# Scaling blocks of probabilities on GpSimd too, with priorities shifted by a fixed table, in an attention and gated feed-forward kernel

## The chip, the cores and the metric

The kernel runs on one core of a Trainium2 chip. The metric is the device time of one execution in microseconds (us), as the median of several runs. A core has TensorE (PE: matmuls and transposes, with PEld for its weight loads), VectorE (DVE), ScalarE (ACT), GpSimd (POOL) and SyncE (SP), which here issues all DMAs. Each engine works through its own list of instructions in order; they meet at semaphores.

## The reference

Windowed causal attention with a linear position bias is followed by a gated feed-forward layer. There are 8 batches of 8 heads, 576 tokens and 64 dimensions a head; then 4608 tokens of 512 go through 1536 hidden channels.

```python
scores = scale * np.matmul(q, k.transpose(0, 1, 3, 2))
mask = (rel >= 0) & (rel < window)               # window = 128
scores = np.where(mask, scores + bias[None], -1000000000.0)
attn = np.exp(scores - np.max(scores, axis=-1, keepdims=True))
attn = attn / (np.sum(attn, axis=-1, keepdims=True) + 1e-09)
attn_out = np.matmul(attn, v)
x = attn_out.transpose(0, 2, 1, 3).reshape(B * S, H * D)
gate = 1.0 / (1.0 + np.exp(-(x @ w_gate)))
out = gate * (x @ w_val) @ w_out
```

## The kernel before

**Attention.** A unit is one batch and one pair of heads, so there are 32 units of 2 x 576 = 1152 tokens, or nine blocks of 128. TensorE computes scores for four blocks at a time (L388), VectorE folds the two halves of the window (L396), adds the bias and takes the minimum of the negated scores (L404), and ScalarE takes the exp with its sum (L407). Three blocks form a group: VectorE adds a small number to the three sums (L422) and takes their reciprocals (L424), and then each of the three 128x128 blocks is multiplied by its own column of reciprocals, on ScalarE (L427) or VectorE (L428). This multiplication is called scaling below. TensorE transposes the three blocks (L432), ScalarE or VectorE copies them out of PSUM (tile both, L205 and L206), and GpSimd spreads them by two selects into pt (L443). After three groups TensorE multiplies with the values (L469 in the first eight units, L493 later), and the result goes to xt and to DRAM; from unit 8 on VectorE adds a second part to it (L505).

**Feed-forward.** All of it runs in pieces that were split into a high and a low part, with three matmuls for a product. A third of the hidden channels is computed while attention runs (gates1, matmul L550, 480 of them); its input x is split from xt or read back (x<-xt, x<-xr), its weights are decoded by ScalarE and VectorE (L303, L304, L307, L215). The rest is done after attention by seven products of combined blocks in place of eight (gates2, L635; mixed inputs cxA, cxB, cxC), and then the output projection (results, L761).

**What sets the order.** Every instruction is first recorded with an engine, a cost, what it reads and writes, and a wanted time (want). `order` then plays the engines forward: of the operations whose inputs are ready it takes the one that can start first, in steps of 0.05 us, and among equals the one with the smaller want. An operation with `ways` may go to another engine at that engine's cost; `port` keeps VectorE and GpSimd from planned work on SBUF at once. The programs are issued in the order of planned starts. In the first 30 us of the plan, gaps of TensorE are filled with matmuls of the identity matrix (L265). The attention operations want a time that advances with the unit (6.5 us each for the first eight, 10 us each later); gates1's matmuls want a million and so fill what is left; scores, transposes and values of unit 8 and later are planned 0.5 us after their inputs. Before the play, `shift` groups the operations by their want and moves some groups:

```python
for seed in SEEDS:
    rnd = random.Random(seed)
    share, width = rnd.choice((5, 20, 60)), rnd.choice((0.7, 2.0, 6.0))
    for group in rnd.sample(groups, max(1, len(groups) // share)):
        shift = rnd.gauss(0.0, width)
```

Of the kernel before, what the change touches and what calls it, by code (L numbers as in the profile page):

```python
# [2 lines left out]

# [47 lines left out]
YIELD = {"DVE": 0.1, "POOL": 0.0}  # L51
NRAW = 2
SOON = 150.0
SEEDS = (36, 163, 243, 291, 310, 1168, 1444)


def as32(ap):
# [7 lines left out]
class Graph:  # L65
# [87 lines left out]
    def shift(self):  # L153

        groups = {}
        for o in self.ops:
            groups.setdefault((o.want, o.seq // 40 if abs(o.want) > 1e5 else 0), []).append(o)
        groups = list(groups.values())
        for seed in SEEDS:
            rnd = random.Random(seed)  # L160
            share, width = rnd.choice((5, 20, 60)), rnd.choice((0.7, 2.0, 6.0))
            for group in rnd.sample(groups, max(1, len(groups) // share)):
                shift = rnd.gauss(0.0, width)
                for o in group:
                    o.want += shift

    def play(self):
        self.fill = []
# [15 lines left out]
def attention_gated_ffn(ctx: ExitStack, tc: tile.TileContext, qd, kd, vd, wg, wv, wo, out):  # L184
    nc = tc.nc
# [230 lines left out]
    def probabilities(u, i0):  # L416
# [8 lines left out]
        for e in range(n):  # L425
            args = lambda e=e: (pb()[:, e], pb()[:, e], st()[:, 6 + e:7 + e])
            g.add("ACT", 0.3, lambda args=args: nc.scalar.mul(*args()), [(kst, 6)], [(kpb, e)], want,  # L427
                  ways=[("DVE", 0.196, True, lambda args=args: nc.vector.tensor_scalar_mul(*args()))])  # L428

        def transpose():  # L430
            for e in range(n):
# [555 lines left out]
```

## Time and profile before

| | |
|---|---|
| median of 3 runs | 974.3 us (974.27 to 975.93) |
| span of the profiled execution | 971.9 us |
| busy share of TensorE, VectorE, ScalarE, GpSimd | 99%, 83%, 54%, 14% |
| attention stage, to the first matmul L635 | 0 to 286.6 us |
| gates2, to the first matmul L761 | 286.6 to 707.6 us |
| results, to the end of TensorE | 707.6 to 968.0 us |
| granted clock of TensorE | 1.00 in every slice |

The profile shows one execution. Its page gives the busy share of each engine; the other views list groups of instructions by line, stretches of time, waits, or the instructions one after another. Durations on ScalarE and VectorE hold a tail that overlaps the next instruction, and ends of matmuls are modelled, so that the distance from one start to the next is the safer price of a matmul.

### The profile page before, as it was taken

To read this page: it belongs to the slowest core of one execution; us is meant where nothing else is said; L and a number is where in the kernel's file an instruction comes from. 1 tells how busy PE (TensorE), PEld (TensorE's weight loads), DVE (VectorE), ACT (ScalarE), POOL (GpSimd) and SP (SyncE) were. 2 spreads that over 40 slices of the span, in tenths; PEclk is the share of its full clock that TensorE was granted. 3 is DMA by queue.
4 is the path that set the end of the run, shared out by engine and by line. 5 is a ranking of instruction groups with operands and counts; after the bars stand their busy time and mean duration, and the time that the engine had idled before them with its cause. 6 is when DMAs were issued, how large, how long until landed. Compare 5 with 4: busy or idle time off the path is not lost.

```text
span 971.9 us, 18577 instructions
## 1 busy us (share of the span) xinstructions
PE 963.7 (99%) x6574; PEld 818.5 (84%) x6574; DVE 808.1 (83%) x1948; ACT 523.9 (54%) x1383; POOL 138.6 (14%) x237
## 2 busy tenths in 40 slices
PE   9999999999999999999999999999999999999998
PEld 7678777777788889999988888888888999988886
DVE  7998989988969998894789439796999779898882
ACT  7999998799945555453444333532463144332320
POOL 5343443234410110000001000010100000000000
PEclk9999999999999999999999999999999999999999
DMA  8776679676635448752154211436345244637101
GB/s 313 223 267 236 226 241 317 213 247 215 221 111 154 168 156 271 227 189 94 50 189 139 100 65 66 140 125 222 102 153 189 93 141 136 228 98 238 44 23 65
DMA packets 83612, 162.68 MB, mean 167 GB/s; under 512 B 9408, under 2 KB 35008, under 8 KB 83520
## 3 DMA queue, kind: packets, MB, share of 16 engines
q1 hardware_dynamic: 83520, 161.51, 49.9%
q8 instruction: 51, 0.84, 0.4%
q14 instruction: 41, 0.34, 0.1%
HBM read 111.15 MB, written 50.33 MB: 166 GB/s over the span
## 4 chain that ended last, share of the span: by engine, by line
PE 87%; DVE 8%; ACT 3%; DMA 1%; issue 1%; POOL 0%; ACTq 0%; POOLq 0%; SPq 0%; DVEq 0%
PE mm L635 40%; PE mm L761 27%; PE mm L550 8%; PE mm L388 5%; PE mm L493 3%; PE mm L432 3%; DVE work L307 1%; ACT pb L407 1%; DMA xr<-xs 1%; DVE pb L404 1%; ACT pb L427 1%; PE mm L469 1%; DVE mm L396 1%; DMA hs<-ring 0%; PE mm L265 0%
## 5 line engine op out<-in xcount | busy, mean ns | idle before, releaser
L635 PE MATMUL mm<-cxB,w2s 128*128 128x512 f32 (+1 forms) x684 | 159.1, 372 | 0.1
L635 PE MATMUL mm<-cxA,w2s 128*128 128x512 f32 (+1 forms) x684 | 159.1, 372 | 0.0
L205 ACT COPY ring<-mm 128x512 f32<-128x512 f32 (+1 forms) x141 | 77.1, 554 | 129.7 <-PE mm L635 101.1
L635 PEld LDWEIGHTS mm<-cxB,w2s 128*128 128x128 f32 x684 | 125.5, 188 | 18.7 <-ACT ring L205 0.5
L635 PEld LDWEIGHTS mm<-cxA,w2s 128*128 128x128 f32 x684 | 125.8, 188 | 18.4
L550 PE MATMUL mm<-x,w 128*128 128x512 f32 x480 | 139.1, 414 | 1.7 <-DVE x L215 1.0
L443 POOL TENSOR_SCALAR_AFFINE_SELECT pt<-both 128x384 f32<-128x384 f32 x192 | 103.6, 564 | 160.8 <-ACT both L205 151.1
L407 ACT ACTIVATE pb<-pb,st 128x128 f32<-128x128 f32 x288 | 112.9, 397 | 9.6 <-DVE st L404 9.2
L761 PE MATMUL mm<-cxA,wos 128*128 128x512 f32 (+1 forms) x540 | 113.7, 367 | 0.0
L761 PE MATMUL mm<-cxB,wos 128*128 128x512 f32 (+1 forms) x540 | 113.3, 367 | 0.0
L761 PEld LDWEIGHTS mm<-cxA,wos 128*128 128x128 f32 x540 | 98.4, 188 | 12.7
L761 PEld LDWEIGHTS mm<-cxB,wos 128*128 128x128 f32 x540 | 98.3, 188 | 12.6
L550 PEld LDWEIGHTS mm<-x,w 128*128 128x128 f32 x480 | 84.4, 188 | 23.6 <-issue 5.3
L646 ACT ACTIVATE sg<-mm 128x512 f32<-128x512 f32 (+1 forms) x96 | 53.9, 564 | 79.7 <-PE mm L635 37.8
L642 DVE TENSOR_TENSOR mm<-mm,ring 128x512 f32<-128x512 f32 (+1 forms) x96 | 62.3, 649 | 31.7 <-PE mm L635 28.2
L214 POOL TENSOR_TENSOR work<-work 128x256 f32<-128x256 f32 x29 | 23.5, 815 | 390.4 <-DVE work L307 282.7
L307 DVE SCALAR_TENSOR_TENSOR work<-work 128x512 int32<-128x512 int32 x104 | 71.5, 701 | 0.6
L427 ACT ACTIVATE pb<-pb,st 128x128 f32<-128x128 f32 x198 | 67.8, 396 | 6.1 <-DVE st L424 5.2
L404 DVE CUSTOM_DVE_ANT_0 pb<-mm,relm 128x128 f32<-128x128 f32 x288 | 67.7, 280 | 0.0
L388 PE MATMUL mm<-kr,qr 64*64 64x192 f32 (+2 forms) x1280 | 67.2, 322 | 0.0
L772 ACT ACTIVATE ring<-mm 128x512 f32<-128x512 f32 (+2 forms) x41 | 22.3, 546 | 82.9 <-PE mm L761 79.7
L388 PEld LDWEIGHTS mm<-kr,qr 64*64 64x64 f32 x1280 | 43.1, 133 | 21.3 <-issue 16.2
(111 smaller groups left out, 1553.8 us busy)
## 6 DMA issues: line engine op xcount, KB each, us to landing
hs<-ring SPq DMA_DIRECT2D x72, 256.0 KB, 2.1
kr<-in_k_dram SPq DMA_DIRECT2D x31, 576.0 KB, 5.0
work<-in_moe_w_gate_dram SPq DMA_DIRECT2D x20, 512.0 KB, 3.9
work<-in_moe_w_val_dram SPq DMA_DIRECT2D x20, 512.0 KB, 4.5
qr<-in_q_dram SPq DMA_DIRECT2D x31, 320.0 KB, 5.4
vr<-in_v_dram SPq DMA_DIRECT2D x32, 288.0 KB, 3.5
xs<-xt SPq DMA_DIRECT2D x32, 288.0 KB, 3.2
hr<-hs SPq DMA_DIRECT2D x18, 512.0 KB, 4.7
```

What stands on the lines that cost most here:

```text
L205: g.add("ACT", act_cost(n, psum), lambda: nc.scalar.copy(out(), src()), reads, writes, want, release=release, ways=[("DVE", dve_cost(n, ps ...
L307: g.add("DVE", dve_cost(DM, two=True), lambda word=word, scalar=scalar, o0=o0: nc.vector.scalar_tensor_tensor(bits(), wraw(s)[:, :, word], ...
L388: nc.tensor.matmul(sp[j // 2][col, j % 2, c0:c0 + n], qraw(u)[row, i // 2, col], kraw(u)[row, k1:k1 + n], start=True, stop=True)
L404: g.add("DVE", 0.21, lambda: nc.vector.tensor_tensor_reduce(pb()[:, e], sp[j // 2][:, j % 2, D:D + P], relm[u.p][:, w], op0=ALU.add, op1=A ...
L407: g.add("ACT", 0.39, lambda: nc.scalar.activation(pb()[:, e], pb()[:, e], AF.Exp, bias=st()[:, e:e + 1], scale=-1.0, accum_out=st()[:, 3 + ...
L427: g.add("ACT", 0.3, lambda args=args: nc.scalar.mul(*args()), [(kst, 6)], [(kpb, e)], want, ways=[("DVE", 0.196, True, lambda args=args: n ...
L443: nc.gpsimd.affine_select(pt(u)[:, f0:f0 + 2 * n - 1:2, :], both(), [[0, n], step], cmp, 0.0, base=0, channel_multiplier=mult)
L550: nc.tensor.matmul(mm[s][:, 0:n], w1(kind, wi)[:, i, c * P:(c + 1) * P], x1(x)[:, c, 0:n], start=(k == 0 and c == 0), stop=(k == 2 and c = ...
L635: nc.tensor.matmul(mm[b][:, 0:N], w2t(i, wp)[:, wk, c * P:(c + 1) * P], combo(k, xp)[:, c, 0:N], start=(start and c == 0 and j == 0), stop ...
L642: g.add("DVE", dve_cost(N, psum=True), lambda: nc.vector.tensor_tensor(o(), bk(b)(), a(), op=ALU.add), [("mm", b), *reads] if okeys else r ...
L646: g.add("ACT", act_cost(N, psum=True), lambda: nc.scalar.activation(sg[h](), bk(b)(), AF.Tanh, scale=0.5), [("mm", b)], [("sg", h)], F)
L761: nc.tensor.matmul(mm[banks_[i]][:, a:b], wot(e * HC + c, wp)[:, k, i * P:(i + 1) * P], hcombo(s, xp)[:, c, a:b], start=(start and e == c ...
```

## The change

Two things change. A scaling may also be planned on GpSimd, at a cost of 0.42 us in the plan, where ScalarE has 0.3 and VectorE 0.196. And `shift` moves the groups by a fixed table of tenths of a microsecond in place of the draws.

```diff
-SEEDS = (36, 163, 243, 291, 310, 1168, 1444)
+SHIFTS = (
+    (2, -27), (3, 4), (4, -5), (5, -4), (6, -10), (7, 3), (8, 7), (9, 13), (10, 11), (12, -44), (14, -3), (15, -8), (16, 5), (17, -56), (18, 4),
...
-        for seed in SEEDS:
-            rnd = random.Random(seed)
-            share, width = rnd.choice((5, 20, 60)), rnd.choice((0.7, 2.0, 6.0))
-            for group in rnd.sample(groups, max(1, len(groups) // share)):
-                shift = rnd.gauss(0.0, width)
-                for o in group:
-                    o.want += shift
+        for k, tenths in SHIFTS:
+            for o in groups[k]:
+                o.want += tenths / 10
...
             g.add("ACT", 0.3, lambda args=args: nc.scalar.mul(*args()), [(kst, 6)], [(kpb, e)], want,
-                  ways=[("DVE", 0.196, True, lambda args=args: nc.vector.tensor_scalar_mul(*args()))])
+                  ways=[("DVE", 0.196, True, lambda args=args: nc.vector.tensor_scalar_mul(*args())),
+                    ("POOL", 0.42, True, lambda args=args: nc.gpsimd.tensor_scalar_mul(*args()))])
```

What this does to the programs is shown at three places. In the new kernel the lines of this part are 18 or 19 higher: selects are L462, scalings L445 (ScalarE), L446 (VectorE) and L447 (GpSimd), exps L425, gates1's matmuls L569, gates2's L654.

GpSimd in the first two units: pb is a block of probabilities, st its sums and reciprocals, both the transposed group, pt the spread one. Before:

```order
L443 AFFINE_SELECT pt_270<-both_261 128x3x128 x2
L443 AFFINE_SELECT pt_270<-both_299 128x3x128 x2
L443 AFFINE_SELECT pt_270<-both_329 128x3x128 x2
L443 AFFINE_SELECT pt_404<-both_261 128x3x128 x2
L443 AFFINE_SELECT pt_404<-both_299 128x3x128 x2
L443 AFFINE_SELECT pt_404<-both_329 128x3x128 x2
```

and now:

```order
L447 TENSOR_SCALAR pb_192<-pb_192,st_193 128x128
L462 AFFINE_SELECT pt_262<-both_251 128x3x128 x2
L462 AFFINE_SELECT pt_262<-both_289 128x3x128 x2
L447 TENSOR_SCALAR pb_270<-pb_270,st_271 128x128
L462 AFFINE_SELECT pt_262<-both_334 128x3x128 x2
L462 AFFINE_SELECT pt_372<-both_251 128x3x128 x2
L447 TENSOR_SCALAR pb_307<-pb_307,st_308 128x128
L447 TENSOR_SCALAR pb_318<-pb_318,st_319 128x128
L462 AFFINE_SELECT pt_372<-both_289 128x3x128 x2
L462 AFFINE_SELECT pt_372<-both_334 128x3x128 x2
L447 TENSOR_SCALAR pb_369<-pb_369,st_370 128x128
L447 TENSOR_SCALAR pb_415<-pb_415,st_416 128x128
```

Scalings of later units stand between the selects of the older ones. The new program has 88 of them on GpSimd.

ScalarE in the first units: exps (L407, now L425), scalings (L427, now L445) and copies of transposed groups. Before, from the first scaling of unit 2 on:

```order
L427 ACTIVATE pb_302<-pb_302,st_303 128x128 x2
L427 ACTIVATE pb_311<-pb_311,st_312 128x128 x2
L407 ACTIVATE pb_364,st_365<-pb_364,st_365 128x128
L205 COPY both_299<-mm_146 128x384
L407 ACTIVATE pb_415,st_416<-pb_415,st_416 128x128 x3
L427 ACTIVATE pb_311<-pb_311,st_312 128x128
L427 ACTIVATE pb_364<-pb_364,st_365 128x128 x3
L205 COPY both_329<-mm_146 128x384
L427 ACTIVATE pb_415<-pb_415,st_416 128x128
L407 ACTIVATE pb_192,st_462<-pb_192,st_462 128x128 x3
L407 ACTIVATE pb_200,st_472<-pb_200,st_472 128x128
L427 ACTIVATE pb_415<-pb_415,st_416 128x128 x2
```

and now, at the same place:

```order
L445 ACTIVATE pb_307<-pb_307,st_308 128x128
L445 ACTIVATE pb_318<-pb_318,st_319 128x128 x2
L223 CAST x_413<-xt_394 128x512
L223 COPY both_289<-mm_146 128x384
L425 ACTIVATE pb_369,st_370<-pb_369,st_370 128x128
L425 ACTIVATE pb_415,st_416<-pb_415,st_416 128x128 x3
L223 COPY both_334<-mm_146 128x384
L445 ACTIVATE pb_369<-pb_369,st_370 128x128
L425 ACTIVATE pb_192,st_458<-pb_192,st_458 128x128 x3
L425 ACTIVATE pb_200,st_467<-pb_200,st_467 128x128
L445 ACTIVATE pb_369<-pb_369,st_370 128x128
L445 ACTIVATE pb_415<-pb_415,st_416 128x128 x2
```

Of scalings there are 198 before and 151 now. In this stretch ScalarE also has a cast of x from xt, which VectorE did. VectorE has 90 scalings before and 49 now.

TensorE at the end of attention, from the last matmuls of the last values on (pt, vr), over the remaining matmuls of gates1 (x, w) to the first of gates2 (cxA). Before:

```order
L493 MATMUL mm_146<-pt_404,vr_180 64x64 x4
L550 MATMUL mm_141<-x_396,w_524 128x512 x12
L550 MATMUL mm_140<-x_396,w_524 128x512 x7
L550 MATMUL mm_141<-x_396,w_524 128x512 x4
L550 MATMUL mm_140<-x_396,w_524 128x512 x12
L550 MATMUL mm_141<-x_396,w_524 128x512 x8
L635 MATMUL mm_140<-cxA,w2s_2461 128x512 x6
L635 MATMUL mm_143<-cxA,w2s_2626 128x512 x6
L635 MATMUL mm_146<-cxA,w2s_4146 128x512 x6
```

and now:

```order
L512 MATMUL mm_146<-pt_372,vr_180 64x64 x4
L569 MATMUL mm_141<-x_413,w_527 128x512 x3
L569 MATMUL mm_140<-x_413,w_527 128x512 x6
L569 MATMUL mm_141<-x_413,w_527 128x512 x12
L569 MATMUL mm_140<-x_413,w_527 128x512 x6
L654 MATMUL mm_143<-cxA,w2s_2707 128x512 x6
L569 MATMUL mm_140<-x_413,w_527 128x512 x12
L569 MATMUL mm_141<-x_413,w_527 128x512 x12
L654 MATMUL mm_140<-cxA,w2s_2507 128x512 x6
L654 MATMUL mm_142<-cxA,w2s_2507 128x512 x6
```

The first six matmuls of gates2 moved ahead of the last 24 of gates1. There are 51 matmuls of gates1 behind the last values now, and there were 43; over the whole stage the 480 stand in 97 runs now and in 106 before, and 33 identity matmuls stand in the program where 32 stood.

## Rows read from the trace of the kernel before

**Rows 1.** the page, engines' busy time over the whole span.
```profile
PE 963.7 (99%) x6574; PEld 818.5 (84%) x6574; DVE 808.1 (83%) x1948; ACT 523.9 (54%) x1383; POOL 138.6 (14%) x237
```

**Rows 2.** Stretches: us; busy PE, PEld, DVE, ACT, POOL (instructions); clock; DMA share; GB/s.
```profile
0.00:50.00 50.00, 47.47 (x497) 35.62 (x498) 43.19 (x212) 42.82 (x168) 22.09 (x41) 1.00 0.80 269
50.00:287.00 237.00, 235.43 (x2799) 185.08 (x2798) 211.41 (x980) 209.06 (x790) 88.62 (x166) 1.00 0.69 229
287.00:708.00 421.00, 420.78 (x2011) 367.49 (x2011) 338.86 (x525) 187.46 (x320) 27.88 (x32) 1.00 0.44 145
```

**Rows 3.** timeline, TensorE and VectorE, attention's end: start, length, what.
```profile
276.60 10.17 PE L550 MATMUL mm<-x,w 128*128 128x512 f32 x43
286.61 2.65 PE L635 MATMUL mm<-cxA,w2s 128*128 128x512 f32 x11
...
279.99 0.69 DVE L206 CAST cxC<-xr 128x1024 fp32r<-128x1024 f32 x1 [2.18 <-DMA xs<-xt]
```

**Rows 4.** groups of TensorE in 0 to 50 us: busy, mean ns, idle before.
```profile
L265 PE MATMUL mm<-ident 128*128 128x128 f32 x64 | 9.2, 284 | 0.0
L270 PE MATMUL mm<-ident 128*128 128x128 f32 x12 | 2.9, 434 | 1.4 <-POOL ident masks.py:199 1.4
```

**Rows 5.** stretch of 25 to 50 us, columns as in rows 2.
```profile
25.00:50.00 25.00, 23.89 (x251) 16.32 (x250) 23.45 (x110) 24.11 (x96) 9.57 (x18) 1.00 0.73 229
```

**Rows 6.** waits of the attention stage: who for whom, us, times, longest.
```profile
PEld mm L432 <- ACT both L205: 2.1, 6, 0.7
PEld mm L469 <- POOL pt L443: 0.6, 2, 0.4
POOL pt L443 <- ACT both L205: 151.1, 83, 9.9
```

**Rows 7.** timeline of TensorE: start, length, what.
```profile
19.00 0.55 PE L432 MATMUL mm<-ident,pb 128*128 128x128 f32 x3
19.47 0.88 PE L388 MATMUL mm<-kr,qr 64*64 64x192 f32 x16
...
213.85 1.62 PE L550 MATMUL mm<-x,w 128*128 128x512 f32 x6
215.31 0.49 PE L432 MATMUL mm<-ident,pb 128*128 128x128 f32 x3
215.56 0.47 PE L550 MATMUL mm<-x,w 128*128 128x512 f32 x1
215.96 0.88 PE L388 MATMUL mm<-kr,qr 64*64 64x192 f32 x16
```

**Rows 8.** groups by line and shape, whole span: busy, mean ns, idle before.
```profile
L427 ACT ACTIVATE pb<-pb,st 128x128 f32<-128x128 f32 x198 | 67.8, 396 | 6.1 <-DVE st L424 5.2 <-DVE st L422 0.7
L205 ACT CAST x<-xr 128x512 fp32r<-128x512 f32 x6 | 3.7, 611 | 0.0
...
L428 DVE TENSOR_SCALAR pb<-pb,st 128x128 f32<-128x128 f32 x90 | 24.0, 302 | 0.2
L422 DVE TENSOR_SCALAR st<-st 128x3 f32<-128x3 f32 x96 | 20.6, 215 | 7.9 <-ACT pb L407 6.7
L206 DVE CAST w<-work 128x512 fp32r<-128x512 f32 x8 | 3.6, 459 | 0.0
...
L443 POOL TENSOR_SCALAR_AFFINE_SELECT pt<-both 128x384 f32<-128x384 f32 x192 | 103.6, 564 | 160.8 <-ACT both L205 151.1 <-DVE both L206 4.6 <-PE mm L388 4.2
L248 POOL TENSOR_SCALAR relm<-relm 128x640 f32<-128x640 f32 x3 | 5.4, 1812 | 1.9 <-DVE relm L243 1.7
```

**Rows 9.** L422's and L428's durations; pairs of selects on GpSimd.
```profile
L422 DVE TENSOR_SCALAR st<-st x96: 134/169/509, 8.2 to 267.2; 128x3 f32<-128x3 f32 x96
...
L428 DVE TENSOR_SCALAR pb<-pb,st x90: 250/277/622, 10.2 to 267.9; 128x128 f32<-128x128 f32 x90
...
56.69 1.00 POOL L443 TENSOR_SCALAR_AFFINE_SELECT pt<-both 128x384 f32<-128x384 f32 x2 [0.93 <-ACT both L205]
59.72 1.33 POOL L443 TENSOR_SCALAR_AFFINE_SELECT pt<-both 128x384 f32<-128x384 f32 x2 [2.04 <-ACT both L205]
```

More of the change, by code (lines that the diff above doesn't have):

```diff
@@ L1 @@
-import random
 from contextlib import ExitStack
@@ L53 @@
 SOON = 150.0
-SEEDS = (36, 163, 243, 291, 310, 1168, 1444)
+SHIFTS = (
[22 rows of a table added]
+)
 def as32(ap):
```

21 rows, old and new, of the table SHIFTS are left out of this document.

## The prediction

> **What bounds the kernel now.** I read the page's busy shares first: TensorE 99% of the span, VectorE 83%, ScalarE 54%, GpSimd 14% [rows 1]. A busy TensorE need not be a working one, so next comes the table by stage [rows 2]. From 286.6 us on (the first F matmul, L635, [rows 3]) there is one kind of work: from 287 to 708 us TensorE idles 0.2 us at the full granted clock. The change neither adds nor removes a matmul there, so these 685 us stay, whatever the order ahead of them. What can move is the stage before, in which 32 units of attention run beside the first 480 matmuls of the feed-forward part (L550, "G" below), each 0.23 us: 43 in a row take from 276.60 to 286.61 [rows 3].
>
> How much slack has that stage? From 0 to 50 us TensorE idles 50 - 47.47 = 2.5 us [rows 2], and of its busy time 9.2 us are identity matmuls that the planner puts into gaps, and 2.9 us those at the start [rows 4]. Of these 14.7 us the first 4.3 (1.4 us of idle and the 2.9) are start-up that the change doesn't touch; 10.4 us are gaps that a better supply could close. From 50 to 287 us the idle time is 237 - 235.43 = 1.6 us. A gain over 12 us is impossible, and the first 50 us decide.
>
> Who makes those gaps? From 25 to 50 us ScalarE is busy 24.1 of 25 us and VectorE 23.5, GpSimd 9.6 [rows 5]. In the list of waits GpSimd stands idle 151 us for ScalarE's copies of transposed blocks, and TensorE's weight loads for transposes (L432) wait for ScalarE [rows 6]. So ScalarE and VectorE are what TensorE lacks early, and GpSimd has room. Later the G matmuls fill what attention leaves open.
>
> **The change part by part.**
>
> *Turns of TensorE.* In the new order the 480 G stand in 97 runs, before in 106; 46 runs end at transposes (51 before), 44 at scores (49). A run that ends at a transpose costs little more than its matmuls: six G start at 213.85 and the transpose at 215.31, 1.46 us against 6 x 0.23 = 1.38, so 0.08. One that ends at scores: one G at 215.56, scores at 215.96, 0.40 against 0.23, so 0.17 [rows 7]. Five fewer of each: -5 x 0.25 = -1.3 us. But a transpose followed by scores (20 times, before 16) holds TensorE 0.47 us (19.00 to 19.47), one followed by G 0.25 (215.31 to 215.56) [rows 7]: +4 x 0.22 = +0.9. Sum -0.4; bounds -1.3 (nothing given back) and 0.
>
> *Blocks moved to GpSimd.* Of the 288 scalings ScalarE had 198 and VectorE 90 [rows 8]; now 151, 49 and 88 on GpSimd. To see what that gives where it matters, I count in both orders what stands on an engine ahead of a given unit's result (the add L505).
>
> - Ahead of unit 10's, TensorE has the same scores but 108 G for 118, 2.3 us less. ScalarE has 27 scalings fewer at 67.8 / 198 = 0.34 us, -9.2, but six casts and copies more of 0.6 us that were VectorE's, +3.6: -5.6 us. VectorE has ten scalings fewer at 24.0 / 90 = 0.27 us, -2.7, and eight casts and copies of about 0.4 us fewer, -3.2: -5.9 us [rows 8]. Both are some 3.4 us ahead of TensorE.
> - Ahead of unit 8's, ScalarE has 19 scalings fewer (-6.5) but five casts and three copies more (+4.6) and four exps (+1.4, priced as scalings): -0.5 us. TensorE has 10 scores more and one G less, +0.6. The lead is 1.1 us there.
>
> So the lead comes late, when most gaps are behind. Bounds: 0, if the gaps of the first units stay, and 5.2, half of the 10.4, if the two engines cause them all and get half of it back. I take the middle of 1.1 and 3.4, -2.2 us, and a quarter of the 1.6 us after 50 us, -0.4.
>
> *Price on GpSimd.* The trace has no scaling of 128x128 by GpSimd. The nearest rows: the same operation on 128x640 takes 1.81 us, and a select over 128x384 0.56 [rows 8]. A fifth of the first, 0.36, leaves out what an instruction costs by itself; the second has three times the columns. Between these I take 0.5, as the fixed part must be added to the first. 88 x 0.5 = 44 us lifts GpSimd from 139 to 183 us, all of it in the first 277, so it does not become the bound. But it works in order. Behind a scaling stand the selects (L443) of an older unit, which TensorE's values wait for, 0.5 us later each; in the trace these waits are 0.6 us in all [rows 6], so the selects come early and hide it. Ahead, a scaling that takes 0.5 in place of 0.34 us holds the group's transposes if it is the last of its three, and on TensorE everything queues behind the transposes. The planner asks half a microsecond of slack there from unit 8 on; the 26 scalings of the first eight units have none. Bounds: 0, and 26 x 0.16 = 4.2 us if each is last and nothing else fills. I take 0, as two engines' relief stands against it in the same place.
>
> *Price on VectorE.* One small instruction of VectorE (L422) takes 0.13 us at best, 0.17 in the median and 0.51 at worst, and a pair of GpSimd's selects 1.00 or, beside VectorE's work, 1.33 [rows 9]. By means against medians L422 loses 96 x (0.215 - 0.169) = 4.4 us and, with 0.277 as its median, L428 90 x (0.302 - 0.277) = 2.3 us: 6.7 us against 104 us of selects [rows 8, 9], 0.064 for each us. Some 37 scalings stand ahead of unit 10, 18 us of GpSimd, so 1.2 us of VectorE; I put half on the path, as ScalarE is as scarce: +0.6 us. Bounds 0 and 1.2.
>
> The Trainium skill ("SBUF — State Buffer", section "Who interferes with whom") says that VectorE and GpSimd have one port pair, locked for a whole instruction, so that one of the two fully waits. The pair of 1.33 for 1.00 agrees in direction; a full wait behind VectorE's long instructions is the rival "lock".
>
> *The end of attention.* Behind the last values 51 G are left (before 43), and the first six F matmuls now stand after 27 of them. They need cxA, whose memory is attention's until its last store: in the trace VectorE is let in at 279.99, 3.4 us after the last values end (276.60) [rows 3]. In the new order VectorE then does two casts (some 0.6 us each) and a subtraction (1.1): the high part is ready 4.0 us, the low part 5.7 us after the values, and TensorE comes after 27 x 0.23 = 6.2. Cost nothing, with 0.5 us of cover; without it at most 1 us, as 24 G queue behind.
>
> **Sum.** -0.4 - 2.2 - 0.4 + 0.6 = -2.4 us. The profiled span is 971.9 us; the runs' median is 974.3, so 2.4 us lie around it, which stay. 974.3 - 2.4 = 971.9 us. Under 0.2% (1.9 us) a difference can't be told from none here.
>
> **Rivals.**
> - *Level.* The early gaps come from the first units' chain (scores, exp, sum, transpose), which no helper shortens. For it: the new order puts 33 identity matmuls into gaps where it put 32, so its early gaps look alike. Against it: both engines are full from 25 us on. Turns and the port remain: -0.4 + 0.2, 974.1 us.
> - *Lock* (slower). GpSimd's scalings wait behind VectorE's instructions on the weights and hold transposes, and with them TensorE's queue. If the 26 without slack cost their whole 4.2 us, the port its 1.2, and the lead gives only unit 8's 1.1 and the 0.4 after, it is -0.4 + 4.2 + 1.2 - 1.5 = +3.5, less the 1.0 that G fill in: 976.8 us. It decides from a mean of about 0.8 us for a scaling, or 3 us of TensorE's waits for it. Against it: GpSimd idles before most of its work [rows 6]. The Trainium skill's "Perfetto Trace Analysis" ("Optimizing Scalar/DVE Operations") warns likewise that moving work from VectorE to GpSimd might not help, for the common port.
> - *Full lead.* The gaps close by half: -0.4 - 5.2 = 968.7 us. For it: by the end both engines are some 10 us lighter; against it: most of that comes after 100 us, where hardly a gap is left.
> - *No helper.* The change might leave GpSimd unused; the order shows 88 blocks there, so this is out.
>
> **How the numbers follow.** Forecast (970.3 to 973.2) 0.42; level 0.23; lock 0.20; full lead 0.15. Faster by over 0.2%: full lead and three quarters of the forecast, 0.15 + 0.32 = 0.47. Slower: most of lock, 0.18, and 0.03 of level: 0.21. Same: 0.32. The range runs from 968.0, just past the full lead, to 976.8, the lock's time.
>
> **What would show it.** First F matmul near 286.6 - 2.4 - 24 x 0.23 = 278.7 us, later stages as long as before. Identity matmuls and idle time of 0 to 50 us fall from 14.7 to some 12.5 us. A scaling on GpSimd takes 0.4 to 0.6 us. Wrong: TensorE waiting over 3 us for GpSimd's scalings, L422's mean well over 0.25 us, over 1 us between the G and the first F, or the gain somewhere after 287 us.

## The result and the profile after

| | before | after |
|---|---|---|
| median (range), 4 runs each | 974.45 us (974.27 to 975.93) | 980.55 us (980.29 to 983.45) |
| ratio, 95% interval | | 1.0062 [1.0044, 1.0081] |
| span of the profiled execution | 971.9 us | 978.9 us |

The change made the kernel 0.6% slower, where 0.25% faster was forecast, and 980.55 us lies outside the range of 968.0 to 976.8. The page's busy shares after, as [rows 1]:

```profile
PE 965.2 (99%) x6576; PEld 817.6 (84%) x6576; DVE 797.1 (81%) x1894; ACT 519.5 (53%) x1345; POOL 206.4 (21%) x329
```

GpSimd does more, VectorE and ScalarE less, as planned, and TensorE is 99% busy in a span 7 us longer. The stretches after, columns and bounds of [rows 2]:

```profile
0.00:50.00 50.00, 46.63 (x502) 36.50 (x503) 42.21 (x204) 42.61 (x163) 32.23 (x53) 1.00 0.78 268
50.00:287.00 237.00, 234.16 (x2789) 182.80 (x2788) 206.93 (x944) 200.46 (x748) 136.35 (x241) 1.00 0.68 227
287.00:708.00 421.00, 417.72 (x1990) 362.76 (x1989) 331.42 (x515) 182.26 (x314) 32.44 (x32) 1.00 0.44 145
```

All three stretches lost some busy time, and the last, which had idled 0.2 us, now idles 3.3 at the same clock. TensorE's timeline after, at the end of attention, as [rows 3]:

```profile
276.22 6.42 PE L569 MATMUL mm<-x,w 128*128 128x512 f32 x27
282.47 1.52 PE L654 MATMUL mm<-cxA,w2s 128*128 128x512 f32 x6
283.83 5.60 PE L569 MATMUL mm<-x,w 128*128 128x512 f32 x24
289.27 1.98 PE L654 MATMUL mm<-cxA,w2s 128*128 128x512 f32 x8
```

The last G end at 289.3. Six F stand ahead of them, so the like-for-like end of attention is 289.3 - 6 x 0.227 = 287.9, against 286.6: +1.3 us. What follows takes 978.9 - 287.9 = 691.0 us against 971.9 - 286.6 = 685.3: +5.7. The greater part was lost where the prediction had excluded any change.

Busy time does not show that loss in full, as ends of matmuls are modelled. So I also use distances between starts: the six F of 512 columns take from 282.47 to 283.83, 0.227 us each, and twelve of 384 columns from 409.55 to the next start at 411.63, 0.173 us each. What a distance has beyond that is called a **gap** below. Summed over the F stage, gaps are 0.8 us before and 6.1 after; in the results stage 0.0 in both. The Trainium skill ("Perfetto Trace Analysis", section "Identifying the Most-Contended Engine") says that matmul busy time is no good measure of how close TensorE is to its limit, and to take its share of peak arithmetic and the busy share of weight loads instead. The first half agrees (99% in both); weight loads, 84% of either span, show the 6 us no better here.

For whom TensorE waits behind attention (287 to 716 us; us in total, times, longest). The same view of before has no such row:

```profile
PE mm L654 <- ACT ring L223: 1.5, 2, 0.9
PE mm L654 <- DVE ring L661: 1.4, 2, 1.0
PE mm L654 <- DVE ring L669: 0.5, 1, 0.5
```

The largest gap after, 1.2 us, lies between the twelve matmuls that start at 415.60 and the next at 418.88. The timeline of the engines there:

```profile
415.60 2.24 PE L654 MATMUL mm<-cxB,w 128*128 128x384 f32 x12
415.61 0.56 DVE L661 TENSOR_TENSOR mm<-mm,ring 128x384 f32<-128x384 f32 x1
415.97 1.84 POOL L232 TENSOR_TENSOR cxB<-xr,cxB 128x768 fp32r<-128x768 f32 x1 [46.88 <-ACT cxB L223]
416.07 2.29 DVE L325 SCALAR_TENSOR_TENSOR work<-work 128x512 int32<-128x512 int32 x1
...
418.29 0.54 DVE L661 TENSOR_TENSOR ring<-mm,ring 128x384 f32<-128x384 f32 x1
...
418.88 0.30 PEld L654 LDWEIGHTS mm<-cxC,w2s 128*128 128x128 f32 x2 [1.36 <-DVE ring L661]
```

VectorE decodes weights for a later product (L325), which takes 2.29 us, where the one at 412.31 took 0.69, while GpSimd subtracts (L232). The addition that frees TensorE's PSUM bank (L661) stands behind it, and TensorE waits. The Trainium skill ("SBUF — State Buffer", section "Who interferes with whom") says that VectorE and GpSimd share one port pair, which an instruction that uses it holds as a whole; 2.29 us, of which 1.74 run beside the 1.84 of GpSimd, agree with a wait for the rest of that instruction. Whether that collision is the cause is asked of e5.

The rows that answer to [rows 4, 8]: identity matmuls of 0 to 50 us, then the scalings and L440 (before L422) over the whole span:

```profile
L283 PE MATMUL mm<-ident 128*128 128x128 f32 x66 | 9.4, 287 | 0.0
L288 PE MATMUL mm<-ident 128*128 128x128 f32 x12 | 2.9, 434 | 1.4 <-POOL ident masks.py:199 1.4
```

```profile
L447 POOL TENSOR_SCALAR pb<-pb,st 128x128 f32<-128x128 f32 x88 | 58.5, 673 | 32.8 <-DVE st L442 24.2 <-ACT x L223 5.0 <-ACT xt L223 1.5
L445 ACT ACTIVATE pb<-pb,st 128x128 f32<-128x128 f32 x151 | 53.2, 396 | 11.4 <-DVE st L442 10.4
...
L440 DVE TENSOR_SCALAR st<-st 128x3 f32<-128x3 f32 x96 | 21.9, 229 | 10.1 <-ACT pb L425 9.0
...
L446 DVE TENSOR_SCALAR pb<-pb,st 128x128 f32<-128x128 f32 x49 | 13.3, 302 | 0.2
```

And waits of the attention stage, as [rows 6]:

```profile
POOL pt L462 <- ACT both L223: 60.1, 57, 4.8
...
PEld mm L451 <- POOL pb L447: 1.0, 2, 0.7
...
PEld mm L512 <- POOL pb L447: 0.4, 1, 0.4
```

### The profile page after: what moved, and what is told of

The parts are those of the page before. It is cut to its first block, busy times and chain, and to the rows that moved or that the text cites. A ratio compares the mean times of both kernels' runs of the same rounds, so it can differ in the third digit from the quotient of the medians.

```text
span 978.9 us, 18550 instructions
## 1 busy us (share of the span) xinstructions
PE 965.2 (99%) x6576; PEld 817.6 (84%) x6576; DVE 797.1 (81%) x1894; ACT 519.5 (53%) x1345; POOL 206.4 (21%) x329
## 4 chain that ended last, share of the span: by engine, by line
PE 77%; DVE 14%; ACT 5%; issue 2%; DMA 2%; POOL 0%; ACTq 0%; DVEq 0%; POOLq 0%
PE mm L654 33%; PE mm L780 26%; PE mm L569 7%; PE mm L406 4%; PE mm L512 3%; PE mm L451 3%; ACT pb L425 2%; DVE work L325 2%; DMA hs<-ring 2%; DVE ring L669 1%; DVE mm L414 1%; DVE mm L661 1%; DVE w2s L233 1%; ACT pb L445 1%; DVE cxA L233 1%
## 5 line engine op out<-in xcount | busy, mean ns | idle before, releaser
L654 PE MATMUL mm<-cxB,w2s 128*128 128x512 f32 (+1 forms) x684 | 158.5, 373 | 2.1 <-ACT ring L223 1.5
L654 PE MATMUL mm<-cxA,w2s 128*128 128x512 f32 (+1 forms) x684 | 158.5, 372 | 0.1
L654 PEld LDWEIGHTS mm<-cxB,w2s 128*128 128x128 f32 x684 | 125.3, 188 | 22.1 <-ACT ring L223 2.7
L654 PEld LDWEIGHTS mm<-cxA,w2s 128*128 128x128 f32 x684 | 125.5, 188 | 19.1 <-DVE w2s L233 0.6
L569 PE MATMUL mm<-x,w 128*128 128x512 f32 x480 | 136.9, 413 | 2.1 <-DVE x L233 1.1
L462 POOL TENSOR_SCALAR_AFFINE_SELECT pt<-both 128x384 f32<-128x384 f32 x192 | 104.3, 568 | 69.7 <-ACT both L223 60.1
L425 ACT ACTIVATE pb<-pb,st 128x128 f32<-128x128 f32 x288 | 112.7, 395 | 10.2 <-DVE st L422 9.7
L569 PEld LDWEIGHTS mm<-x,w 128*128 128x128 f32 x480 | 84.3, 188 | 22.2 <-DVE x L233 3.7
L661 DVE TENSOR_TENSOR mm<-mm,ring 128x512 f32<-128x512 f32 (+1 forms) x96 | 61.8, 648 | 40.6 <-PE mm L654 34.4
L232 POOL TENSOR_TENSOR work<-work 128x256 f32<-128x256 f32 x28 | 26.7, 970 | 320.3 <-DVE work L325 219.5
L325 DVE SCALAR_TENSOR_TENSOR work<-work 128x512 int32<-128x512 int32 x104 | 70.3, 703 | 0.5
L422 DVE CUSTOM_DVE_ANT_0 pb<-mm,relm 128x128 f32<-128x128 f32 x288 | 67.8, 279 | 0.1
L447 POOL TENSOR_SCALAR pb<-pb,st 128x128 f32<-128x128 f32 x88 | 58.5, 673 | 32.8 <-DVE st L442 24.2
L414 DVE COPY_PREDICATED mm<-swap,mm 128x256 f32<-128x256 int32 x144 | 56.2, 419 | 11.3 <-PE mm L406 10.9
## 6 DMA issues: line engine op xcount, KB each, us to landing
vr<-in_v_dram SPq DMA_DIRECT2D x32, 288.0 KB, 3.9
xs<-xt SPq DMA_DIRECT2D x32, 288.0 KB, 3.4
```

Of the source, the lines that this page charges most:

```text
L325: g.add("DVE", dve_cost(DM, two=True), lambda word=word, scalar=scalar, o0=o0: nc.vector.scalar_tensor_tensor(bits(), wraw(s)[:, :, word], ...
L414: g.add("DVE", dve_cost(4 * D, psum=True), lambda b=b: nc.vector.copy_predicated(fold[b][:, :, 1:3], swaps, fold[b][:, :, 3::-3]), [], [(" ...
L422: g.add("DVE", 0.21, lambda: nc.vector.tensor_tensor_reduce(pb()[:, e], sp[j // 2][:, j % 2, D:D + P], relm[u.p][:, w], op0=ALU.add, op1=A ...
L425: g.add("ACT", 0.39, lambda: nc.scalar.activation(pb()[:, e], pb()[:, e], AF.Exp, bias=st()[:, e:e + 1], scale=-1.0, accum_out=st()[:, 3 + ...
L447: ("POOL", 0.42, True, lambda args=args: nc.gpsimd.tensor_scalar_mul(*args()))])
L462: nc.gpsimd.affine_select(pt(u)[:, f0:f0 + 2 * n - 1:2, :], both(), [[0, n], step], cmp, 0.0, base=0, channel_multiplier=mult)
```

## The experiments

The change has two parts, and the table acts in two places: on the attention stage's groups, and on TensorE's products behind attention. These too have wants, all one million. A count over the list of groups (486 in all) gives: of the 47 groups of products behind attention the table shifts 35, the old draws shifted 4; of the 122 groups of ScalarE's, VectorE's and SyncE's work for the feed-forward part the table shifts none, the draws 21.

Theories: (A) the old draws on those 122 groups are lost; (B) GpSimd's scalings take longer than planned (0.60 us from start to start for 0.42); (C) the table's shifts of attention are to blame; (D) the order behind attention is worse, whatever precedes it; (E) any mixture of plans stalls; (F) VectorE and GpSimd block each other. D divides later into (P) the table's shifts of products and (Q) the other engines' order.

In this table "end" is attention's like-for-like end and "gaps" those of the F stage, both from the one profiled execution; the ratios are to the kernel before on the same chip.

| run | median us | ratio, interval | end | gaps |
|---|---|---|---|---|
| e1 GpSimd alone, draws kept | 978.39 | 1.0039 [1.0025, 1.0052] | 288.7 | 2.5 |
| e2 table alone | 989.29 | 1.0154 [1.0138, 1.0170] | 291.4 | 10.8 |
| e3 after + old draws on the 122 groups | 983.92 | 1.0093 [1.0078, 1.0107] | 287.3 | 9.3 |
| e4 GpSimd scales 56 of 128 columns | 981.54 | 1.0068 [1.0054, 1.0082] | 287.0 | 7.1 |
| e5 late subtractions on VectorE | 982.49 | 1.0084 [1.0063, 1.0105] | 287.0 | 11.2 |
| e6 new attention, old order behind it | 977.19 | 1.0033 [1.0021, 1.0044] | 289.2 | 1.9 |
| e7 old attention, new order behind it | 986.93 | 1.0139 [1.0123, 1.0155] | 289.3 | 11.1 |
| e8 light decoding | 976.67 | 1.0027 [1.0016, 1.0037] | 287.2 | 2.9 |
| e9 light stores | 980.19 | 1.0056 [1.0041, 1.0071] | 287.6 | 3.9 |
| e10 both light | 976.05 | 1.0014 [1.0005, 1.0024] | 286.9 | 2.7 |
| e11 after without shifts of late products | 976.40 | 1.0018 [1.0009, 1.0028] | 288.0 | 2.4 |
| e12 price 0.60 in the plan | 985.51 | 1.0117 [1.0101, 1.0132] | 291.0 | 6.9 |
| e13 before + shifts of late products | 981.35 | 1.0076 [1.0046, 1.0105] | 286.4 | 6.4 |
| e14 as e11, GpSimd below unit 8 | 978.68 | 1.0043 [1.0028, 1.0058] | 289.9 | 2.0 |
| e15 as e11, GpSimd below unit 16 | 975.17 | 1.0006 [0.9996, 1.0016] | 287.4 | 1.8 |

Gaps of one execution scatter: e5's profiled execution was the longest of its four (984.72 of 978.96 to 984.72), e9's the shortest (977.93 of 977.93 to 980.78). Where gaps and median disagree, I go by the median.

**One part alone (e1, e2).** e1 takes the changed kernel and puts the draws back; e2 takes GpSimd's way out:

```diff
-        for k, tenths in SHIFTS:
-            for o in groups[k]:
-                o.want += tenths / 10
+        for seed in SEEDS:
...
```

```diff
-                  ways=[("DVE", 0.196, ...),
-                    ("POOL", 0.42, True, lambda args=args: nc.gpsimd.tensor_scalar_mul(*args()))])
+                  ways=[("DVE", 0.196, ...)])
```

> The draws of before are kept and only the GpSimd way for scalings is added. Theory A (the loss lies behind attention, where the table has no shift for the operations on ScalarE, VectorE and SyncE that the draws had shifted): TensorE's stalls between 290 and 716 us return from 6.1 to under 2 us, attention ends some 1 to 3 us later than in the kernel before; 975 to 977 us. Theory B (a scaling takes 0.60 us on GpSimd where the plan has 0.42, and everything slips): about as slow as the changed kernel, 979 to 981 us. Theory C (the table's shifts of attention are to blame): as fast as before, 974 to 975 us.

> The fixed table, but scalings on ScalarE and VectorE alone. Theory A: the stalls behind attention stay at 4 us or more, 978 to 980 us. Theory B: with no scaling on GpSimd the loss goes, 974 us or less. Theory C: 979 to 981 us, with attention's end at 288 us or later.

Each part alone loses, and the table without GpSimd loses more than both together: the effects do not add. e1 came out between A and B, e2 far above every theory. Behind attention the table goes with gaps of 10.8 us, GpSimd's way without it with 2.5, where the kernel before has 0.8.

**The lost draws (e3).**

```diff
+        late = [g for g in groups if g[0].want < -1e5]
+        for seed in (36, 163, 243, 291, 310, 1168, 1444):
...
+                    o.want += shift * (group in late)
```

> The changed kernel, with the old draws put back for the groups wanted first (their want is about minus a million: ScalarE, VectorE and SyncE work of the feed-forward part), which the table leaves alone. Attention keeps the table and GpSimd's scalings. Theory A: the last L569 ends near 289 us as in the changed kernel, but the stalls of TensorE behind it fall from 6.1 to under 2 us: 975 to 977 us. Theories B and C: nothing of the loss goes, 979 to 981 us.

Slower still, so A falls: giving these draws back to another plan only gives a third order.

**Same order, one duration less (e4, e5).** In both, the planned order is the changed kernel's; e5 issues two of GpSimd's instructions to VectorE instead, at the same place.

```diff
-                    ("POOL", 0.42, True, lambda args=args: nc.gpsimd.tensor_scalar_mul(*args()))])
+                    ("POOL", 0.42, True, lambda e=e: nc.gpsimd.tensor_scalar_mul(pb()[:, e, 0:56], pb()[:, e, 0:56], ...))])
```

```diff
-        way = ("POOL", ..., lambda: nc.gpsimd.tensor_tensor(out(), a(), b(), op=ALU.subtract))
+        way = ("POOL", ..., lambda: (nc.vector if n > 512 else nc.gpsimd).tensor_tensor(out(), a(), b(), op=ALU.subtract))
```

> The changed kernel in its own order, but GpSimd scales only 56 of a block's 128 columns (the other 72 stay unscaled), so that one takes about 0.43 us, near the plan's 0.42, not 0.60. Theory A: attention ends 1 to 2 us sooner, the stalls behind it stay over 4 us: 978 to 980 us. Theory B: the loss goes, 974 to 976 us. Theory C: no change, 980 us.

> The changed kernel in its own order; only the two subtractions of 128x768 that the plan gives to GpSimd behind attention (cxA and cxB) run on VectorE, at the same place of the order. Theory F (GpSimd and VectorE hold each other up behind attention): the stall of 1.2 us at 417 us goes with VectorE's 2.29 us instruction there, and those behind it with it, so 977 to 979 us. Theory D (VectorE's work behind attention stands in an order in which a finished block is late for its store, which holds a slot of the ring, ScalarE's copy, a PSUM bank and TensorE): at most that one stall goes, others remain, 979 to 981 us.

The group of e4's scalings:

```profile
L447 POOL TENSOR_SCALAR pb<-pb,st 128x56 f32<-128x56 f32 x88 | 40.7, 475 | 36.5 <-DVE st L442 25.4 <-DVE st L422 3.7 <-ACT x L223 2.9
```

A mean of 475 in place of 673 ns bought no time (981.54). The end at 287.0 looks like a gain of 0.9 us, but e5, e8, e9, e10 and e11, whose attention is that of the changed kernel, end it at 286.9 to 288.0; so B isn't shown. In e5 the collision is gone: VectorE's L325 of 419.10 takes 0.68 us, and TensorE goes from the twelve matmuls on to the next product without a wait. The median gains nothing, but e5 is no clean test of F, as VectorE now does the two subtractions itself. Its profiled execution also lost time just ahead of that place:

```profile
416.39 0.66 ACT L321 ACTIVATE work<-work 128x512 f32<-128x512 f32 x1 [2.84 <-DMA wod<-work]
...
417.47 1.34 PE L654 MATMUL mm<-cxB,w2s 128*128 128x384 f32 x6 [2.52 <-ACT ring L223]
...
418.65 3.81 PE L654 MATMUL mm<-cxB,w 128*128 128x384 f32 x12
419.10 0.68 DVE L325 SCALAR_TENSOR_TENSOR work<-work 128x512 int32<-128x512 int32 x1
...
422.29 1.20 PE L654 MATMUL mm<-cxC,w2s 128*128 128x384 f32 x6
```

```profile
418.00:423.00 5.00, 5.00 (x22) 5.00 (x21) 4.56 (x10) 1.41 (x3) 0.00 (x0) 0.66 0.71 222
```

ScalarE waits for a store, TensorE for ScalarE, a gap of 2.7 us. Soon after it TensorE's granted clock falls: 0.66 in the mean from 418 to 423 us, which is 1.2 in place of 2.4 GHz for 3.4 us, and twelve matmuls take 3.64 us (418.65 to 422.29) for the usual 2.08. So 1.6 of e5's 11.2 us of gaps are clock. So of F this much is shown: the collision makes one gap of 1.2 us in 6.1, and those after it, 0.65 us at 439.6 and 1.1 at 460.6 in the changed kernel, are still there in e5 without it. GpSimd's 28 subtractions of 128x256 (970 ns in the mean, 815 in the kernel before) stayed where they were, so for these F is not tested.

**Grafts (e6, e7).** Both plans are made, operations up to the end of attention are issued in the order of the one and the rest in the order of the other:

```diff
+        early, fill = self.plan(False)   # e7: True
+        late, _ = self.plan(True)        # e7: False
...
+            one = early if o.seq < self.cut else late
```

> A graft: every operation that is recorded up to the end of attention keeps the changed kernel's plan (table, GpSimd's scalings), every later one has the plan of the kernel before, shifted as a whole so that the last early matmul of TensorE stands at the same place. Theory D (the loss lies in the late order itself): TensorE's stalls behind attention are under 1.5 us, attention ends 1 us later or so, 974 to 976 us. Theory E (a late order fits only the early one with which it was planned): stalls of over 3 us, 978 to 981 us.

> The other graft: attention as in the kernel before, everything later in the changed kernel's plan. Theory D: attention ends as before (286.6 us) and the stalls behind it are 4 us or more: 978 to 980 us. Theory E: also over 3 us of stalls, as both grafts mix two plans; only e6 tells D and E apart. If the early part alone were to blame, it would be 974 to 975 us.

With the old late order gaps are 1.9 us although another attention precedes it; with the new one 11.1, part of them at the seam (4.1 us from 281 to 307; two waits of the seam, 0.8 and 0.9 us, are also in e7's end of 289.3). e6 misses D's bounds by a little (1.9 us for 1.5, 977.19 us for 976) and E's by more (over 3 us, 978), so D is borne out and E is not. e7, at 986.93, is 7 us above the 978 to 980 expected, of which the waits of the seam make about 5.

**Late work made light (e8, e9, e10).** The order stays the changed kernel's. What is left out stands in the expectations.

```diff
+        m = 128 if late else DM
-                bits(), wraw(s)[:, :, word], scalar, bits(), op0=o0, op1=ALU.bitwise_or), ...
+                bits()[:, 0:m], wraw(s)[:, 0:m, word], scalar, bits()[:, 0:m], op0=o0, op1=ALU.bitwise_or), ...
```

```diff
+            d = a + 64 if late else e
-            move(lambda b=b, a=a, e=e: hs[k][b][c][:, a - EDGE[b]:e - EDGE[b]], lambda a=a, e=e: src()[:, a - t0:e - t0],
+            move(lambda b=b, a=a, d=d: hs[k][b][c][:, a - EDGE[b]:d - EDGE[b]], lambda a=a, d=d: src()[:, a - t0:d - t0],
```

> The changed kernel in its own order, but behind attention VectorE's two instructions that put each weight block together (L325) write 128 of 512 columns, so each takes some 0.2 in place of 0.6 us (weights behind attention are then not put together fully). Theory D: VectorE is no longer late, the waits of ScalarE's ring copies for stores fall well below 42.7 us and TensorE's stalls behind attention from 6.1 to under 2 us: 974 to 976 us. If the ring's six slots and the stores' own time are the limit, whatever VectorE does: over 4 us of stalls, 979 to 981 us.

> The changed kernel in its own order on every engine, with 64 columns in place of 384 or 512 in each of the stores of the hidden channels that are made behind attention (hs from ring; the loads behind them read another tensor of the same shape). Theory (the new late order leaves TensorE's next inputs too little lead, and two things use it up: late VectorE work and stores that hold a slot of the ring): ScalarE's waits for these stores fall from 42.7 us to under 10, TensorE's stalls behind attention from 6.1 to about 3.5 us, the rest being VectorE's; time 977 to 978.5 us. Rival (VectorE's lateness is the one cause, and the ring is late only because of it): stalls stay at 5 to 6 us, 979.5 to 981 us. Rival (the stores take the DMA engines' time from the loads): stalls under 1 us, 975 to 976 us.

> The changed kernel in its own order, with both edits: the two decoding instructions of VectorE behind attention write 128 of 512 columns, and the stores from the ring behind attention write 64 columns. Theory (late VectorE work and held ring slots together are the whole of the late loss): stalls behind attention under 1.2 us, as before the change (0.8); attention's own 1.3 us stay, so 975 to 976 us. Rival (a third thing, TensorE's turn of products or ScalarE, makes the rest): stalls of 2.5 us or more are left, 976.5 to 977.5 us, no better than the light decode alone (976.7).

ScalarE's waits for stores from the ring, 287 to 716 us, after and then in e8:

```profile
ACT ring L223 <- DMA hs<-ring: 42.7, 25, 4.6
```

```profile
ACT ring L223 <- DMA hs<-ring: 43.0, 22, 5.1
```

Two of the three decoding instructions in a quarter of the columns (77 of 705 ns become 76 of 287, so 33 us less for VectorE) win 3.9 us and leave these waits as they are, though the theory had them fall; the instruction made short is also that of the collision, so e8 does not tell D from F. Short stores cut the waits to 25.0 us (31.4 with both) and win nothing in the median (980.19 against 980.55). So my theory of two causes is half wrong: the time that the new order lacks is mostly VectorE's, and most waits of a ring slot cost nothing. One does. Of the 2.7 us of gaps that e10 keeps, 1.2 are at 456.6 us, where ScalarE's copy into the ring waits for a store although the store is short:

```profile
456.12 0.48 ACT L223 COPY ring<-mm 128x384 f32<-128x384 f32 x1 [2.64 <-DMA hs<-ring]
456.65 0.65 PEld L656 LDWEIGHTS mm<-cxB,w2s 128*128 128x128 f32 x4 [1.34 <-ACT ring L223]
```

The changed kernel has that gap at 460.6 (1.1 us, behind a wait of 2.57), and e8 at 457.2. Another 1.1 us of e10's gaps, at 435.6 and 709.7, stand behind VectorE's additions and products (L663, L671).

**The shifts of products (e11, e13).** e11 leaves those shifts out of the changed kernel, e13 puts them alone into the kernel before, in place of its draws on the same groups (every engine's later order is planned anew in both):

```diff
         for k, tenths in SHIFTS:
             for o in groups[k]:
-                o.want += tenths / 10
+                if o.want < 5e5 or o.seq < self.cut:
+                    o.want += tenths / 10
```

```diff
-                    o.want += shift
+                    if not (o.want > 5e5 and o.seq >= self.cut):
+                        o.want += shift
+        for k, tenths in SHIFTS:
+            for o in groups[k]:
+                if o.want > 5e5 and o.seq >= self.cut:
+                    o.want += tenths / 10
```

> The changed kernel without the table's shifts on groups of TensorE's products behind attention (46 groups at most); attention's order is word for word the changed kernel's, up to the first mixed products. Theory P (these shifts pull single products ahead or back without their inputs being pulled with them): stalls behind attention fall from 6.1 to under 2.5 us, 976 to 977.5 us. Theory Q (what is lost are the old draws' few shifts on VectorE's and ScalarE's late work, and TensorE's order only follows): stalls stay at 5 us or more, 979.5 to 982 us. Rival (the play is so sensitive that any list of shifts that was not picked out loses there): also 5 us or more, and up to 11, 980 to 986 us.

> The kernel before, its draws kept and no scaling on GpSimd, with the new table's shifts on one kind of group alone: TensorE's products behind attention (the draws' shifts on those groups are left out). Attention's order is word for word the old one up to the first mixed products. Theory P (these shifts pull products out of turn and lose by themselves): TensorE's stalls behind attention rise from 0.8 to 4 us or more, 978 to 986 us. Rival (they lose only with the new plan's late state, or the plain order of products was a lucky one): stalls under 2.5 us, 974 to 976.5 us.

Both come out as P says. Taken out, 980.55 becomes 976.40 with attention's order unchanged; put in alone, 974.16 becomes 981.35, attention's end stays (286.4), and gaps go from 0.8 to 6.4. Of e13's four executions two take 979.2 and 979.3 us, and two, with a mean granted clock of 0.998 and 0.997, 983.4 and 985.0; so 5 of the 7.2 us stand without a fall of the clock. TensorE's products after, from 403 us on:

```profile
403.31 2.24 PE L654 MATMUL mm<-cxA,w 128*128 128x384 f32 x12
405.39 1.20 PE L654 MATMUL mm<-cxC,w2s 128*128 128x384 f32 x6
406.43 2.24 PE L654 MATMUL mm<-cxA,w 128*128 128x384 f32 x12
408.51 1.20 PE L654 MATMUL mm<-cxA,w2s 128*128 128x384 f32 x6
409.55 2.24 PE L654 MATMUL mm<-cxB,w2s 128*128 128x384 f32 x12
```

and in e11:

```profile
403.46 1.20 PE L655 MATMUL mm<-cxA,w2s 128*128 128x384 f32 x6
404.50 1.20 PE L655 MATMUL mm<-cxC,w2s 128*128 128x384 f32 x6
405.54 1.20 PE L655 MATMUL mm<-cxB,w2s 128*128 128x384 f32 x6
406.58 1.20 PE L655 MATMUL mm<-cxA,w 128*128 128x384 f32 x6
407.62 1.20 PE L655 MATMUL mm<-cxB,w2s 128*128 128x384 f32 x6
408.66 1.20 PE L655 MATMUL mm<-cxA,w 128*128 128x384 f32 x6
409.70 1.20 PE L655 MATMUL mm<-cxB,w2s 128*128 128x384 f32 x6
```

A chunk of hidden channels has seven products, three on cxA, three on cxB and one on cxC, each with a copy, an addition or a tanh behind it. In e11 two chunks run staggered, so that here the kinds alternate; after, that pattern is broken, and products of one kind stand in twos. The loss itself is shown by the two runs; how the broken pattern makes it is not. Products of one kind in a row are not enough, as the kernel before has four and six of them, 24 and 36 matmuls, with no gap behind them:

```profile
424.12 4.32 PE L635 MATMUL mm<-cxA,w2s 128*128 128x384 f32 x24
428.28 1.20 PE L635 MATMUL mm<-cxB,w2s 128*128 128x384 f32 x6
429.32 1.20 PE L635 MATMUL mm<-cxA,w2s 128*128 128x384 f32 x6
430.36 6.40 PE L635 MATMUL mm<-cxB,w2s 128*128 128x384 f32 x36
436.60 1.20 PE L635 MATMUL mm<-cxC,w2s 128*128 128x384 f32 x6
```

What TensorE waits for in e11 and then in e13, 287 to 716 us:

```profile
PE mm L655 <- ACT ring L224: 0.7, 2, 0.5
```

```profile
PE mm L664 <- ACT sg L675: 2.2, 1, 2.2
PE mm L664 <- ACT ring L234: 1.0, 2, 0.6
PE mm L664 <- DVE ring L671: 0.8, 1, 0.8
```

The table's sizes don't matter there. The key in `order` is the start in steps of 0.05 us, then want, then the place of recording. Products of equal want that can start at once go as recorded; one moved by a tenth goes ahead of, or behind, all the others. With these shifts divided by ten, every engine's program is the same, instruction for instruction.

**Another price (e12).**

```diff
-                    ("POOL", 0.42, True, ...)])
+                    ("POOL", 0.6, True, ...)])
```

> The changed kernel with a cost of 0.60 us in the plan for a scaling on GpSimd (measured: 0.60 from start to start) in place of 0.42; every engine's order is planned anew with the same table. Theory (the plan is late because it prices GpSimd too low): attention ends 0.5 to 1 us earlier than the changed kernel's 287.9 and the stalls behind it fall by some us, 976 to 979 us. Rival (the table fits one play alone, and another price gives another play): attention ends at 288 us or later, stalls behind it of 4 to 11 us, 980 to 989 us.

The measured price makes it worse, as the rival said: attention ends at 291.0, the gaps are 6.9. Of the two prices that ran, the table does better with 0.42.

**GpSimd for early units only (e14, e15).** With e11's edit, and

```diff
+                  ways=[("DVE", ...), ("POOL", 0.42, ...)][:2 if u.n < 8 else 1])   # e15: 16
```

> As plain products (the table's shifts left off TensorE's products behind attention), and GpSimd may scale blocks of the first eight units only (21 blocks); up to there the order is the changed kernel's. Theory (the blocks given to GpSimd later, when the first matmuls of the feed-forward part fill all gaps, cost attention its 0.3 to 1.4 us): attention ends at 285 to 286.8 us, and the time is 973 to 975.5 us, at or under the kernel before. Rival (these blocks do nothing there, and the table fits the plan in which GpSimd has them): attention ends at 288 us or later, 976 to 980 us.

> As the run before, with GpSimd allowed for the first sixteen units (36 blocks). Theory: between the two, attention's end 285.5 to 287.3 us, 973.5 to 976 us. Rival: attention ends at 288 us or later, 976 to 980 us.

GpSimd scales 25 blocks in e14 and 47 in e15, by the counts of their traces, and not the 21 and 36 of the expectations (nor the 26 of the prediction for the first eight units). e14 ends attention at 289.9 and e15 at 287.4, against 288.0 with GpSimd throughout. Fewer blocks are not steadily better, so the theory that late blocks cost attention its time is not borne out. e15, at 975.17, can't be told from the kernel before; no version beat it.

## Why the prediction was wrong

*The step that failed* is "these 685 us stay, whatever the order ahead of them". They became 691.0 in the profiled execution. The reason given, that TensorE idles 0.2 us there and no matmul is added, holds for the number of matmuls and not for their order, and the order behind was changed too: 35 of 47 groups of products. I had followed the new order to the first F and no further, and taken an idle time near zero for slack. It showed a plan without slack: e13, with these shifts alone, turns 0.8 us of gaps into 6.4 and costs 7.2 us. Over all runs with the full late work, the eight with the table's shifts of products (after, e2 to e5, e7, e12, e13) have gaps of 6.1 to 11.2 us, the six without (before, e1, e6, e11, e14, e15) 0.8 to 2.5.

*Turns of TensorE, -0.4 (bounds -1.3 and 0).* By difference: of the +1.3 us at attention's end, +1.0 are idle time and identity matmuls of the first 50 us and +1.2 idle time behind them (next paragraph), which leaves about -0.9; right in sign, within the bounds.

*Blocks moved to GpSimd, -2.2 and -0.4.* This gain did not come. Idle time and identity matmuls of the first 50 us are 3.4 + 9.4 + 2.9 = 15.7 us for 14.7, and from 50 to 287 us TensorE idles 2.8 for 1.6. The blocks moved as counted, and GpSimd's wait for ScalarE's copies fell from 151 to 60 us, but the gaps stayed: here the rival "level" was right. Like-for-like, attention ends at 286.9 to 288.0 in the six profiles with the changed kernel's attention and at 286.4 to 286.6 in two with the old, some 0.9 us later. Which of the 232 shifted attention groups do that stays open: e4, e14 and e15 don't settle it.

*Price on GpSimd, 0.5 us a block at no cost.* It takes 0.60 from start to start where two follow each other unhindered, a fifth more; the mean is 0.673, as some take up to 1.4. TensorE waited 1.0 + 0.4 us for these blocks in the rows above, below the 3 us from which the rival "lock" decides, and e4 finds no price in time. Cost nothing: borne out. Lock's 976.8 came nearest of all the rivals' times, but not by its mechanism.

*Price on VectorE, +0.6 (0 to 1.2).* L440's mean is 229 ns for 215, so 96 x 0.014 = 1.3 us of VectorE over the whole stage, and the scalings left on VectorE still take 302. The rate on record, 0.064 for each us of GpSimd, would give 88 x 0.5 x 0.064 = 2.8 us there, so the rate was about twice too high; what part lies on the path was not separated.

*The end of attention, 0.* TensorE goes from the 27 G to the six F without a wait: 6.25 us from 276.22 to 282.47 are 0.231 for a G, where the 43 of before took 0.233. The first of VectorE's subtractions for them starts at 280.95 and, at 1.22 us, ends some 0.3 us ahead: right, with as little cover as was estimated (0.5).

Had the late stage stayed at 685.3 us, the profiled span would be 287.9 + 685.3 = 973.2 us, +1.3: the forecast's sign would still have been wrong, by the missing gain in the first 50 us.

## What to carry to other kernels

Where a table or a draw sets the order, follow it through every stage, and ask of shifts on equal priorities who now overtakes whom: there a tenth of a microsecond is a rank, not a time. A stage that idles 0.2 us in 421 is no safe stage but one whose order fits; put the order of one stage into the other plan before believing a gain in another. A table of shifts goes with the plan that it shifts: with another price (e12) or without GpSimd's scalings (e2) this one cost 5 and 9 us more.

## What the runs showed of the hardware

A scaling of 128x128 takes GpSimd 601 ns at least, 607 in the median and 673 in the mean; ScalarE takes 396 and VectorE 302 in the mean. A 128x512 decode of VectorE beside a 1.84 us subtraction on GpSimd took 2.29 us, for 0.69 without it. With stores of 64 columns in place of 384 or 512, ScalarE still waited up to 4.6 us for one of them to release its ring slot: in e9 the store was issued at 305.82 and the copy started at 309.88, 4.06 us, and in the changed kernel, with eight times the bytes, 306.17 to 310.21, 4.04. So there the hold is not its bytes.

TensorE's clock can fall behind a gap, and the fall costs time on top of it: e5's profile shows 1.2 GHz for 3.4 us soon after an idle time of 2.5 us, at a price of 1.6 us. It need not fall: behind e7's idle time of 2.3 us, which ends at 297.15, the clock stayed at 1.00. In the eight versions with gaps of 6 us and more, 10 of 33 executions have a mean granted clock of 0.996 to 0.998; in the kernel before, in e1, e6, e8 to e11, e14 and e15 not one has less than 0.999. Of the changed kernel's four it is the one at 983.45 us, where the others take 980.3 to 980.6 at 1.000. Only e5's fall is in a trace, so that the others fell in the same way is not shown.
